# Weight passes tied into program order, and a different start of the first pair, in a one-core attention and two-layer kernel

## The chip, the cores and the metric

The kernel runs on one core of a Trainium2 chip. The metric is the device time of one execution in microseconds (us); lower is better. Five engines work side by side, each through its own list of instructions in a fixed order: TensorE (PE in the profile, its weight loads PEld), VectorE (DVE), ScalarE (ACT), GpSimd (POOL) and SyncE (SP), which here issues every transfer. An instruction whose input is not there yet holds up all that stand behind it in its engine's list.

## The reference

```python
def _attn_ref(q, k, v):                       # 4 batches, 8 heads, 1152 rows, 64 wide
    q_pool = q.reshape(B, H, S // 2, 2, D).mean(axis=3)
    scores = 1.0 / np.sqrt(D) * np.matmul(q_pool, k.transpose(0, 1, 3, 2))
    attn = np.exp(scores - np.max(scores, axis=-1, keepdims=True))
    attn = attn / (np.sum(attn, axis=-1, keepdims=True) + 1e-09)
    return np.matmul(attn, v)                 # 576 rows a head
...
x = attention, laid out as 2304 tokens x 512
h = x @ w_in;   g = h * np.cos(h);                  x = g @ w_out     # 512 x 2048 x 512
h = x @ w_in2;  g = h * (1.0 / (1.0 + np.exp(-h))); return g @ w_out2
```

The weights arrive as 64-bit numbers, q, k and v as 32-bit ones.

## The kernel before

Attention is worked off in 16 pairs of heads, four to a batch. A pair has nine tiles of query rows, so a batch has 36 tiles. Ahead of its tiles, `pair_prep` takes the largest magnitudes of q, k and v (`absmax`, L121 in the profile), makes power-of-two scales from them through a small product with a constant matrix on TensorE (`scale_steps`, tile `bm`, L105 to L116), splits q, k and v into a high and a low half in 16 bits on ScalarE and VectorE (`qn`, `kn`, `vt`; L481 to L485, L436, L441), and has q and k transposed by transfers (`qT`, `kT`). For each tile TensorE makes the scores (`sp`, L521), VectorE copies them out with their minimum (`sc`, L540, two instructions a tile, the first 512 wide; then `nb`, L545), ScalarE takes the exponential (L548) and the high half (`hl`, L554), GpSimd the low half (L559), a transfer transposes both (`hlT`, L561), and TensorE multiplies with v (`pv`, L572 and L576). There are four `sc` buffers, and one comes free when GpSimd has made the low half. After every three tiles VectorE closes a group (`den`, L584).

While the first batch runs, the first layer's weights are prepared in 16 pieces of 1 MB (`layer1_weight_steps`): eight of `w_in`, then eight of `w_out`. A piece is loaded into one of three buffers (`wst`, L180). It has two ScalarE instructions (L196, L197), three VectorE passes over 1024 columns (L198, L202, L206), called weight passes below, a small product for its scale (`mw`, `bm`), two more ScalarE instructions (L219, L220) and one on GpSimd (L221). The next load waits until the third pass has freed its buffer. No first-layer product (`h`, L657) can start before half of the first batch's last pair is through; from then on attention and first layer share the engines. The second layer follows.

The order of each engine's list is set when the program is built: a scheduler issues what it takes to be ready, by a priority that is the place in the code. `W1_TABLE = (6, (0, 2, 4, 8, 11))` says at which steps of the code a piece's parts are written down: piece i at 6i, its parts at the offsets; a tile has four such steps. The scheduler may issue a part earlier than that, when its inputs are there.

```python
s, u = w.si, w.ui                              # one scale a piece
sc = scale_steps(m, pspool(), (s, u), 14, True, True, True)
```

The product tile `bm` comes from a pool of two TensorE accumulation buffers (`ps_h`), which the pairs' scales and the weight pieces' scales share.

Of the kernel before, what the change touches and what calls it, by code (L numbers as in the profile page):

```python
# [26 lines left out]
PSH = 15.0  # L27
# [3 lines left out]
W1_TABLE = (6, (0, 2, 4, 8, 11))  # L31
# [17 lines left out]
def attention_moe_moe_kernel(ctx, tc, q, k, v, w_in1, w_out1, w_in2, w_out2, out):  # L49
# [34 lines left out]
    def scale_steps(m, pool, res, top, wide=False, apart=False, clean=False):  # L84
# [5 lines left out]
        if wide:  # L90
            w = small.tile([128, 1], F32, name="mw", tag="mw")
            wi, mi = w.bitcast(I32), m.bitcast(I32)
            nc.vector.tensor_scalar(
                out=wi, in0=mi, scalar1=3, scalar2=EXP_MASK if clean else 0x3F800000, op0=ALU.logical_shift_left,
                op1=ALU.bitwise_and
            )
# [8 lines left out]
        nc.tensor.matmul(bc[:, 0:n], mean, m, start=True, stop=True)  # L105
# [12 lines left out]
        )  # L118

# [45 lines left out]
    def layer1_weight_steps(w, srcs, stage, pspool, eng, bufs, wt_bufs, period, offs):  # L165
# [20 lines left out]
        def piece_steps(kind, p):  # L186
# [9 lines left out]
            nc.scalar.activation(out=t, in_=hf, func=AF.Abs, scale=2.0**16)  # L196
            nc.scalar.activation(out=low, in_=high16, func=AF.Identity, scale=2.0**-13, bias=floor3)  # L197
            nc.vector.tensor_scalar(  # L198
                out=t, in0=t, scalar1=W_MIN * 2.0**16, scalar2=None, op0=ALU.max, op1=ALU.max, accum_out=m
            )  # L200
            yield
            nc.vector.scalar_tensor_tensor(  # L202
                out=ti, in0=ti, scalar=3, in1=low, op0=ALU.logical_shift_left, op1=ALU.bitwise_or
            )
            yield
            nc.vector.scalar_tensor_tensor(  # L206
                out=ti, in0=st[:, :, :, 1], scalar=-(1 << 31), in1=ti, op0=ALU.bitwise_and, op1=ALU.bitwise_or
            )
# [3 lines left out]
            sc = scale_steps(m, pspool(), (s, u), 14, True, True, True)  # L212
# [17 lines left out]
        for _ in range(bufs):  # L230
            more()
        yield
        events = []
        for i, x in enumerate(pieces):
            g = []
            events += [(i * period + o, len(events) + k, x, g) for k, o in enumerate(offs)]
        events.sort(key=lambda x: x[:2])
        now = 0
        for when, _, x, g in events:
# [3 lines left out]
            if not g:  # L243
                g.append(piece_steps(*x))
# [198 lines left out]
    def pair_prep(at, P):  # L443
# [9 lines left out]
        for i in range(2):  # L453
            absmax(m[:, 3 + i:4 + i], P.v[i], AX.XY)
            yield
        m3 = small.tile([128, 3], F32, name="pm3", tag="pm3")
        nc.vector.tensor_copy(m3[:, 0:1], m[:, 0:1])
        nc.vector.tensor_reduce(
            out=m3[:, 1:3], in_=m[:, 1:5].rearrange("p (a b) -> p a b", b=2), axis=AX.X, op=ALU.max
        )  # L460
# [41 lines left out]
        for i in range(2):  # L502
            do_v(i)
            yield
# [737 lines left out]
```

## Time and profile before

| | before |
|---|---|
| median of 3 runs | 1375.48 us (1375.44 to 1376.28) |
| profiled execution: its own time | 1377.37 us |
| profiled execution: span of the core | 1375.3 us |
| busy share of the span: PE, DVE, ACT, POOL | 84%, 76%, 63%, 45% |
| transfers: share of 16 engines' span | 65% |
| mean granted TensorE clock | 0.917 |

The span runs from the first to the last recorded instruction; the rest of an execution's own time lies around it. Busy shares are means over stages with different limits. The granted clock is a share of full speed (2.4 GHz); the profile shows it per stretch.

### The profile page before, as it was taken

Reading aid. Unit: us, or ns where it says so; the run is one execution under the profiler, and the core shown is the slowest. Engines: PE = TensorE matmul, PEld = TensorE weight load, DVE = VectorE, ACT = ScalarE, POOL = GpSimd, SP = SyncE. Lnnn points to the kernel's source line nnn. Section 1 sums busy time; section 2 is a strip of 40 time slices with the busy share of each in tenths; the row PEclk is TensorE's granted clock in tenths of the full one; section 3 lists DMA queues with packets and bytes.
Section 4 is the critical chain, followed back from the end, with each engine's and each line's share of the span. In section 5 each row is a group of like instructions: output and inputs, shape, how many; then the busy total and the mean of one; then the engine's idle time right before and its main releaser. Section 6 shows DMA issues by size and latency. Waiting matters only on the chain. (4 is left out here: it accounts for less than half of the span.)

```text
span 1375.3 us, 26440 instructions
## 1 busy us (share of the span) xinstructions
PE 1152.2 (84%) x10668; PEld 917.7 (67%) x10668; DVE 1046.8 (76%) x1927; ACT 871.6 (63%) x1061; POOL 624.3 (45%) x352
## 2 busy tenths in 40 slices
PE   1554656888998778888898889998999999999998
PEld 0232334566776556665676668787788888888887
DVE  7799988798887979986898996786757755444483
ACT  4868878578777778886688765634546634433352
POOL 2475867456566465655377553352667500000000
PEclk9756758888999889998999999999999999999999
DMA  9989999987799999998899966422345000000001
GB/s 289 204 160 241 243 210 179 176 166 134 143 212 176 199 195 209 173 164 176 152 198 202 208 116 126 102 91 55 85 93 131 31 24 24 17 16 16 17 31 31
DMA packets 509593, 186.26 MB, mean 135 GB/s; under 512 B 465952, under 2 KB 484384, under 8 KB 509472
## 3 DMA queue, kind: packets, MB, share of 16 engines
q1 hardware_dynamic: 509472, 184.59, 65.0%
q8 instruction: 83, 1.36, 0.4%
q14 instruction: 38, 0.31, 0.1%
HBM read 66.58 MB, written 9.44 MB: 55 GB/s over the span
## 5 line engine op out<-in xcount | busy, mean ns | idle before, releaser
L559 POOL TENSOR_TENSOR hl<-sc,hl 128x1152 f16<-128x1152 f32 x144 | 370.1, 2581 | 170.1 <-ACT hl L554 94.2
L521 PE MATMUL sp<-kT,qT 128*128 128x512 f16 (+1 forms) x768 | 198.3, 377 | 102.8 <-DVE sc L540 91.8
L540 DVE TENSOR_SCALAR_CACHE_REDUCE sc<-sp,psu 128x512 f32<-128x512 f32 (+1 forms) x288 | 228.6, 808 | 48.4 <-PE sp L521 43.4
L657 PEld LDWEIGHTS <-ih 128*128 128x128 f16 x2304 | 226.7, 100 | 44.2 <-issue 12.9
L572 PE MATMUL pv<-vt,hlT 128*128 128x130 f16 (+1 forms) x1440 | 197.9, 239 | 54.0 <-DMA hlT<-hl 45.1
L548 ACT ACTIVATE sc<-sc,nb 128x1152 f32<-128x1152 f32 x144 | 179.7, 1250 | 82.3 <-DVE nb L545 59.2
L572 PEld LDWEIGHTS <-hlT 128*128 128x128 f16 (+1 forms) x1440 | 148.0, 111 | 92.3 <-DMA hlT<-hl 64.4
L657 PE MATMUL h<-ys,ih 128*128 128x256 f16 x1152 | 195.6, 274 | 4.1 <-ACT gs L673 4.1
L521 PEld LDWEIGHTS <-qT 128*128 128x128 f16 x768 | 77.3, 109 | 167.0 <-issue 130.8
L657 PE MATMUL h<-xT,ih 128*128 128x256 f16 x1024 | 187.8, 278 | 0.7 <-DMA xT<-xn 0.6
L576 PE MATMUL pv<-vt,hlT 128*128 128x65 f16 (+1 forms) x1440 | 188.3, 209 | 0.0
L554 ACT ACTIVATE hl<-sc 128x1152 f16<-128x1152 f32 x144 | 164.7, 1154 | 26.7 <-DMA hlT<-hl 13.3
L712 PE MATMUL y<-gh,oh 128*128 128x256 f16 x576 | 162.9, 283 | 7.8 <-ACT y L721 7.1
L712 PE MATMUL y<-gl,oh 128*128 128x256 f16 x576 | 163.0, 283 | 0.4 <-POOL gl L701 0.4
L712 PE MATMUL y<-gh,ol 128*128 128x256 f16 x576 | 162.8, 283 | 0.0
L826 PEld LDWEIGHTS <-op 128*128 128x128 f16 x1512 | 147.9, 98 | 18.0 <-issue 0.6
L657 PE MATMUL h<-ys,il 128*128 128x256 f16 x576 | 157.8, 274 | 0.0
L576 PEld LDWEIGHTS <-hlT 128*128 128x128 f16 (+1 forms) x1440 | 144.7, 109 | 19.3 <-issue 11.4
L657 PE MATMUL h<-xT,il 128*128 128x256 f16 x512 | 141.9, 277 | 0.0
L701 POOL TENSOR_TENSOR gl<-tt,gh 128x1024 f16<-128x1024 f32 x36 | 93.7, 2603 | 92.5 <-DVE gh L700 82.1
L712 PEld LDWEIGHTS <-oh 128*128 128x128 f16 x1152 | 114.9, 102 | 28.5 <-issue 9.6
L657 PEld LDWEIGHTS <-il 128*128 128x128 f16 x1152 | 114.3, 99 | 15.6
(310 smaller groups left out, 2043.3 us busy)
## 6 DMA issues: line engine op xcount, KB each, us to landing
wst<-in_moe_w_in_dram SPq DMA_DIRECT2D x16, 1024.0 KB, 6.2
stk<-in_k_dram SPq DMA_DIRECT2D x32, 288.0 KB, 4.0
stv<-in_v_dram SPq DMA_DIRECT2D x32, 288.0 KB, 4.1
stq<-in_q_dram SPq DMA_DIRECT2D x32, 256.0 KB, 3.2
wst<-in_moe_w_out_dram SPq DMA_DIRECT2D x8, 1024.0 KB, 6.2
wst<-in_moe_w_out_dram SPq DMA_DIRECT2D x16, 512.0 KB, 6.1
ydr<-y SPq DMA_DIRECT2D x9, 512.0 KB, 3.3
y32b<-ydr SPq DMA_DIRECT2D x9, 512.0 KB, 3.3
```

The source lines that it names most:

```text
L521: nc.tensor.matmul(sp[:, o - a:o - a + n], P.qT[e][:, t, :], kT[:, o:o + n], start=(e == 0), stop=(e == 1))
L540: nc.vector.tensor_scalar(out=T.sc[:, a:z], in0=sp, scalar1=T.P.su, scalar2=None, op0=ALU.mult, op1=ALU.min, accum_out=mx[:, x:x + 1],)
L548: nc.scalar.activation(out=T.sc, in_=T.sc, func=AF.Exp, scale=-1.0, bias=nb)
L554: nc.scalar.activation(out=hi, in_=T.sc, func=AF.Copy)
L559: nc.gpsimd.tensor_tensor(out=T.hl[:, 1, :], in0=T.sc, in1=T.hl[:, 0, :], op=ALU.subtract)
L572: nc.tensor.matmul(G.pv[r, T.gi], T.hlT[:, 0, c, r], P.vt[i][:, c], start=(c == 0), stop=(c == KC - 1), skip_group_check=True,)
L576: nc.tensor.matmul(G.pv[r, T.gi, 0], T.hlT[:, 1, c, r], P.vt[i][:, c, 0], start=False, stop=(c == KC - 1), skip_group_check=True,)
L657: nc.tensor.matmul(hp, wt[:, c, f * 128:(f + 1) * 128], xt(c), start=(i == 0), stop=(i == 3 * NC - 1), skip_group_check=True,)
L701: nc.gpsimd.tensor_tensor(out=G.gl, in0=t, in1=gh, op=ALU.subtract)
L712: nc.tensor.matmul(blk.y[:, oc, :], wt[:, f, oc * 128:(oc + 1) * 128], gt[:, f % 4, :], start=(f == 0 and e == 0 and oc % 2 == 0), stop=(f ...
L826: nc.tensor.matmul(bank, t[:, e, c, :], wt[:, c, :], start=start, stop=True, skip_group_check=True)
```

## The change

It has four parts. In the diff, `pin` (the scheduler's `keep_in_program_order`) lets the scheduler issue an instruction only behind the one that was written down just ahead of it for the same engine.

1. A one-element exponential of a constant (`warm`) is issued on ScalarE at the start; the instruction that loads ScalarE's function table then stands in front of it and no longer in front of `qn`.
2. For the first pair alone, v's maxima and scale are taken out of the common scale and get a product of their own (`pmv`, `pmm`, `psv`); q and k's product has two columns instead of three.
3. In front of the first pair, two weight pieces instead of three are started (the new last number of `W1_TABLE`); the third load is written down behind the first pair's preparation.
4. All other parts of the weight pieces, from the scale on for the first two, are pinned.

```diff
-W1_TABLE = (6, (0, 2, 4, 8, 11))
+W1_TABLE = (6, (0, 2, 4, 8, 11), 2)
...
         nc.vector.memset(halfpi, math.pi / 2)
+        nc.scalar.activation(out=small.tile([128, 1], F32, name="warm", bufs=1), in_=halfpi, func=AF.Exp)
...
-        nc.tensor.matmul(bc[:, 0:n], mean, m, start=True, stop=True)
+        put(nc.tensor.matmul(bc[:, 0:n], mean, m, start=True, stop=True))
...
+    pin = tc.keep_in_program_order
...
-            nc.scalar.activation(out=t, in_=hf, func=AF.Abs, scale=2.0**16)
+            put(nc.scalar.activation(out=t, in_=hf, func=AF.Abs, scale=2.0**16))
...
-            sc = scale_steps(m, pspool(), (s, u), 14, True, True, True)
+            sc = scale_steps(m, pspool(), (s, u), 14, True, True, True, pin)
...
-            nc.scalar.activation(out=hi, in_=t, func=AF.Copy, scale=s)
-            nc.scalar.activation(out=t, in_=t, func=AF.Copy, scale=s)
-            nc.gpsimd.tensor_tensor(out=lo, in0=t, in1=hi, op=ALU.subtract)
+            pin(nc.scalar.activation(out=hi, in_=t, func=AF.Copy, scale=s))
+            pin(nc.scalar.activation(out=t, in_=t, func=AF.Copy, scale=s))
+            pin(nc.gpsimd.tensor_tensor(out=lo, in0=t, in1=hi, op=ALU.subtract))
...
-        for _ in range(bufs):
+        for _ in range(first):
             more()
         yield
+        for _ in range(bufs - first):
+            more()
         events = []
         for i, x in enumerate(pieces):
             g = []
-            events += [(i * period + o, len(events) + k, x, g) for k, o in enumerate(offs)]
+            if i < first:
+                g.append(piece_steps(*x, lambda ins: ins))
+                for _ in range(2):
+                    next(g[0])
+            events += [(i * period + o, len(events) + k, x, g) for k, o in enumerate(offs) if i >= first or k >= 2]
+        yield
...
-                g.append(piece_steps(*x))
+                g.append(piece_steps(*x, pin))
...
+        if apart:
+            nc.vector.tensor_reduce(out=m3[:, 1:2], in_=m[:, 1:3], axis=AX.X, op=ALU.max)
+            run_all(scale_steps(m3[:, 0:2], ps_h, (s[:, 0:2], u[:, 0:2]), 12))
...
+        def v_scale():
+            mv = small.tile([128, 2], F32, name="pmv", bufs=1)
+            for i in range(2):
+                absmax(mv[:, i:i + 1], P.v[i], AX.XY)
+            mm = small.tile([128, 1], F32, name="pmm", bufs=1)
+            nc.vector.tensor_reduce(out=mm, in_=mv, axis=AX.X, op=ALU.max)
+            sv_, uv_ = (small.tile([128, 1], F32, name=nm, bufs=1) for nm in ("psv", "puv"))
+            run_all(scale_steps(mm, ps_h, (sv_, uv_), 12))
+            return sv_
...
+        P.sv = v_scale() if apart else sv
...
-                run_all(pair_prep(at, P[0]))
+                run_all(pair_prep(at, P[0], True))
+                next(wg)
```

The changed kernel's lines have higher numbers: L198, L202, L206 become L201, L205, L209, L540 becomes L565, L554 becomes L579, L219 and L220 become L222 and L223. In the built lists the 48 weight passes stand on VectorE, counted between the first score copies (512 wide) of the tiles named, as follows: ahead of tile 0 there were 8 and are now 6; from there to tile 9 (pair one's first) 10 and now 5; to tile 18 (pair two's first) 15 and now 13; to tile 27 (pair three's first) 12 and now 19; behind it 3 and now 5. On SyncE three weight loads still stand in front, in the same place. Of the 16 loads, 7 stood ahead of the transpose of tile 2, 3 more ahead of that of tile 9, 4 more ahead of tile 18's and the last 2 ahead of tile 27's; now it is 5, 2, 5 and 4.

VectorE's list from the first pair to the first score copy, the last twelve rows of before (three weight passes, two L198 and one L202, stand ahead of them, behind the first pair's `vt`):

```order
L121 TENSOR_REDUCE pm<-stk 128x1
L206 SCALAR_TENSOR_TENSOR wt<-wst,wt 128x1024
L108 TENSOR_SCALAR ui_76<-bm 128x1
L202 SCALAR_TENSOR_TENSOR wt<-wt,wst 128x1024
L93 TENSOR_SCALAR mw<-wm 128x1
L198 TENSOR_SCALAR wt,wm<-wt 128x1024
L112 TENSOR_SCALAR si_75<-ui_76 128x1
L206 SCALAR_TENSOR_TENSOR wt<-wst,wt 128x1024
L202 SCALAR_TENSOR_TENSOR wt<-wt,wst 128x1024
L116 TENSOR_SCALAR ui_76<-ui_76 128x1
L93 TENSOR_SCALAR mw<-wm 128x1
L540 TENSOR_SCALAR sc,mx<-sp,psu 128x512
```

The same stretch of VectorE's list in the changed kernel, whole, right behind the first pair's `vt`:

```order
L201 TENSOR_SCALAR wt,wm<-wt 128x1024
L205 SCALAR_TENSOR_TENSOR wt<-wt,wst 128x1024
L201 TENSOR_SCALAR wt,wm<-wt 128x1024
L209 SCALAR_TENSOR_TENSOR wt<-wst,wt 128x1024
L94 TENSOR_SCALAR mw<-wm 128x1
L124 TENSOR_REDUCE pm<-stk 128x1
L205 SCALAR_TENSOR_TENSOR wt<-wt,wst 128x1024
L209 SCALAR_TENSOR_TENSOR wt<-wst,wt 128x1024
L94 TENSOR_SCALAR mw<-wm 128x1
L565 TENSOR_SCALAR sc,mx<-sp,psu 128x512
```

Two passes and the first piece's scale moved behind the first score copy.

ScalarE's list in pair zero, from pair one's splits to the fourth tile's `hl`, before:

```order
L548 ACTIVATE sc<-sc,nb 128x1152
L481 ACTIVATE qn<-stq,ps__293 128x9x64 x2
L436 ACTIVATE kn<-stk,ps__293 128x9x64 x2
L219 ACTIVATE ih_82<-wt,si_75 128x4x256
L436 ACTIVATE vt<-stv,ps__293 128x9x64 x2
L554 ACTIVATE hl<-sc 128x1152
L548 ACTIVATE sc<-sc,nb 128x1152
L219 ACTIVATE ih_82<-wt,si_75 128x4x256 x2
L197 ACTIVATE wst<-wst,floor_74 128x1024
L548 ACTIVATE sc<-sc,nb 128x1152
L220 ACTIVATE wt<-wt,si_75 128x1024
L554 ACTIVATE hl<-sc 128x1152
```

The same stretch of ScalarE's list in the changed kernel:

```order
L505 ACTIVATE qn<-stq,ps__270 128x9x64 x2
L446 ACTIVATE kn<-stk,ps__270 128x9x64 x2
L446 ACTIVATE vt<-stv,ps__270 128x9x64 x2
L579 ACTIVATE hl<-sc 128x1152
L222 ACTIVATE ih_82<-wt,si_75 128x4x256
L573 ACTIVATE sc<-sc,nb 128x1152
L222 ACTIVATE ih_82<-wt,si_75 128x4x256
L573 ACTIVATE sc<-sc,nb 128x1152
L223 ACTIVATE wt<-wt,si_75 128x1024
L579 ACTIVATE hl<-sc 128x1152
```

Five weight instructions stood there and three do now; up to the fourth `hl`, counted from the list's start, 17 did and 7 do now.

VectorE's list near the change from pair two to pair three, before (tile 26's copies and the start of pair four's maxima):

```order
L540 TENSOR_SCALAR sc,mx<-sp,psu 128x512
L198 TENSOR_SCALAR wt,wm<-wt 128x1024
L540 TENSOR_SCALAR sc,mx<-sp,psu 128x640
L202 SCALAR_TENSOR_TENSOR wt<-wt,wst 128x1024
L93 TENSOR_SCALAR mw<-wm 128x1
L545 TENSOR_SCALAR nb<-mx 128x1
L206 SCALAR_TENSOR_TENSOR wt<-wst,wt 128x1024
L121 TENSOR_REDUCE pm<-stk 128x1
L121 TENSOR_REDUCE pm<-stv 128x1
L108 TENSOR_SCALAR uo_78<-bm 128x1
L121 TENSOR_REDUCE pm<-stv 128x1
L112 TENSOR_SCALAR so_77<-uo_78 128x1
```

VectorE's list in the changed kernel, twelve rows out of the 37 between tile 26's last score copy and tile 27's first (`pu__1358` and `ps__1357` are pair three's scales):

```order
L201 TENSOR_SCALAR wt,wm<-wt 128x1024
L205 SCALAR_TENSOR_TENSOR wt<-wt,wst 128x1024
L209 SCALAR_TENSOR_TENSOR wt<-wst,wt 128x1024
L94 TENSOR_SCALAR mw<-wm 128x1
L109 TENSOR_SCALAR uo_78<-bm 128x1
L113 TENSOR_SCALAR so_77<-uo_78 128x1
L109 TENSOR_SCALAR pu__1358<-bm 128x3
L117 TENSOR_SCALAR uo_78<-uo_78 128x1
L113 TENSOR_SCALAR ps__1357<-pu__1358 128x3
L117 TENSOR_SCALAR pu__1358<-pu__1358 128x3
L480 TENSOR_SCALAR psu<-pu__1358 128x1
L506 SCALAR_TENSOR_TENSOR qn<-stq,ps__1357,qn 128x9x64
```

Pair three's scale now stands behind a weight piece's scale, and its splits stand behind all of pair two's score copies; before, its splits (`qn`, `kn`) stood among the copies of tiles 25 and 26. Pair two's splits moved in the same way, from the copies of tiles 12 to 14 to behind tile 17's. In this stretch of 37 rows stand ten weight passes.

## Rows read from the trace of the kernel before

**Rows 1.** Busy time by stretch: length, PE, PEld, DVE, ACT, POOL, clock, DMA share, GB/s.

```profile
0.00:29.77 29.77, 3.25 (x10) 1.90 (x11) 20.14 (x38) 14.07 (x15) 4.99 (x15) 1.00 0.94 274
29.77:85.77 56.00, 27.09 (x144) 14.69 (x144) 46.56 (x102) 38.66 (x40) 31.30 (x13) 0.72 0.80 190
85.77:145.66 59.89, 31.33 (x265) 20.39 (x264) 55.35 (x114) 51.19 (x56) 38.81 (x19) 0.67 1.12 237
145.66:196.29 50.63, 33.55 (x277) 21.46 (x275) 46.06 (x107) 42.60 (x48) 33.40 (x20) 0.67 1.11 228
196.29:234.43 38.14, 23.32 (x190) 14.10 (x190) 33.60 (x79) 28.66 (x36) 30.09 (x14) 0.77 0.92 175
234.43:262.20 27.77, 20.77 (x216) 13.34 (x214) 23.77 (x61) 19.98 (x22) 19.69 (x13) 0.81 1.05 205
262.20:1057.00 794.80, 701.15 (x6724) 553.47 (x6724) 641.21 (x1170) 541.88 (x659) 447.51 (x245) 0.94 0.78 154
1057.00:1375.30 318.30, 311.69 (x2853) 278.33 (x2850) 180.06 (x267) 134.52 (x187) 18.48 (x17) 1.00 0.07 23
```

**Rows 2.** Timeline of the first pair: start, duration, engine, instruction, [idle before, releaser].

```profile
9.03 1.45 DVE L121 TENSOR_REDUCE pm<-stv 128x1 f32<-128x576 f32 x2
...
10.73 0.59 PE L105 MATMUL bm<-pm,mean 128*128 128x3 f32 x2 [10.73 <-DVE pm L458]
11.36 0.16 DVE L108 TENSOR_SCALAR pu__151<-bm 128x3 f32<-128x3 f32 x1 [0.68 <-PE bm L105]
11.55 0.17 DVE L112 TENSOR_SCALAR ps__150<-pu__151 128x3 int32<-128x3 int32 x1
...
11.79 1.28 ACT L481 ACT_TABLE_LOAD   x1 [11.79 <-DMA wst<-in_moe_w_in_dram]
...
13.08 1.44 ACT L481 ACTIVATE qn<-stq,ps__150 128x576 f16<-128x576 f32 x2
13.89 0.82 DVE L482 SCALAR_TENSOR_TENSOR qn<-stq,ps__150,qn 128x576 f16<-128x576 f32 x1 [1.72 <-ACT qn L481]
...
19.74 2.73 SPq L497 DMA_TRANSPOSE kT<-kn  x1
...
24.39 2.08 PE L521 MATMUL sp<-kT,qT 128*128 128x512 f16 x6 [2.89 <-DMA kT<-kn]
...
27.30 2.43 DVE L202 SCALAR_TENSOR_TENSOR wt<-wt,wst 128x1024 int32<-128x1024 int32 x1
...
29.77 0.73 DVE L540 TENSOR_SCALAR_CACHE_REDUCE sc<-sp,psu 128x512 f32<-128x512 f32 x1
```

**Rows 3.** Groups of instructions on VectorE, 0 to 262 us: weight passes.

```profile
L202 DVE SCALAR_TENSOR_TENSOR wt<-wt,wst 128x1024 int32<-128x1024 int32 x16 | 29.9, 1866 | 0.3 <-DVE uo L108 0.2
L206 DVE SCALAR_TENSOR_TENSOR wt<-wst,wt 128x1024 int32<-128x1024 int32 x16 | 28.9, 1804 | 0.0
L198 DVE TENSOR_SCALAR_CACHE_REDUCE wt<-wt 128x1024 f32<-128x1024 f32 x16 | 19.3, 1208 | 0.0
```

**Rows 4.** Timeline of pair zero, 54 to 70 us, all engines.

```profile
54.10 2.17 ACT L219 ACTIVATE ih<-wt,si 128x1024 f16<-128x1024 f32 x2
...
61.66 2.18 ACT L220 ACTIVATE wt<-wt,si 128x1024 f32<-128x1024 f32 x2
...
64.44 0.22 DVE L584 TENSOR_SCALAR den<-pv,ps__150 128x3 f32<-128x3 f32 x1 [6.49 <-PE pv L576]
...
67.39 4.21 POOL L221 TENSOR_TENSOR il<-wt,ih 128x1024 f16<-128x1024 f32 x2
...
69.55 0.74 DVE L540 TENSOR_SCALAR_CACHE_REDUCE sc<-sp,psu 128x512 f32<-128x512 f32 x1
```

**Rows 5.** Timeline of SyncE, one transpose, about 113 us.

```profile
113.09 6.61 SPq L487 DMA_TRANSPOSE qT<-qn  x1
```

**Rows 6.** Timelines of GpSimd and VectorE, 71 to 83 us.

```profile
71.56 11.32 POOL L559 TENSOR_TENSOR hl<-sc,hl 128x1152 f16<-128x1152 f32 x4
...
77.38 3.27 DVE L206 SCALAR_TENSOR_TENSOR wt<-wst,wt 128x1024 int32<-128x1024 int32 x1
```

More of the change, by code (lines that the diff above doesn't have):

```diff
@@ L163, in new_w, with layer1_weight_steps @@
         return w
-    def layer1_weight_steps(w, srcs, stage, pspool, eng, bufs, wt_bufs, period, offs):
+    def layer1_weight_steps(w, srcs, stage, pspool, eng, bufs, wt_bufs, period, offs, first):
         npc = w.npc
@@ L184, in more, with piece_steps @@
             staged.append(st)
-        def piece_steps(kind, p):
+        def piece_steps(kind, p, put):
             st = staged.pop(0)
@@ L195, in piece_steps @@
             high16 = st.rearrange("p c f z -> p c (f z)").bitcast(U16).rearrange("p c (f z) -> p c f z", z=4)[:, :, :, 1]
[L196 to L198 removed]
+            put(nc.scalar.activation(out=t, in_=hf, func=AF.Abs, scale=2.0**16))
+            put(nc.scalar.activation(out=low, in_=high16, func=AF.Identity, scale=2.0**-13, bias=floor3))
+            put(nc.vector.tensor_scalar(
                 out=t, in0=t, scalar1=W_MIN * 2.0**16, scalar2=None, op0=ALU.max, op1=ALU.max, accum_out=m
[L200 removed]
+            ))
             yield
[L202 removed]
+            put(nc.vector.scalar_tensor_tensor(
                 out=ti, in0=ti, scalar=3, in1=low, op0=ALU.logical_shift_left, op1=ALU.bitwise_or
[L204 removed]
+            ))
             yield
[L206 removed]
+            put(nc.vector.scalar_tensor_tensor(
                 out=ti, in0=st[:, :, :, 1], scalar=-(1 << 31), in1=ti, op0=ALU.bitwise_and, op1=ALU.bitwise_or
[L208 removed]
+            ))
             more()
@@ L452, in pair_prep @@
         yield
-        for i in range(2):
-            absmax(m[:, 3 + i:4 + i], P.v[i], AX.XY)
-            yield
+        s = small.tile([128, 3], F32, name="ps_", tag="ps_", bufs=3)
+        u = small.tile([128, 3], F32, name="pu_", tag="pu_", bufs=3)
         m3 = small.tile([128, 3], F32, name="pm3", tag="pm3")
         nc.vector.tensor_copy(m3[:, 0:1], m[:, 0:1])
-        nc.vector.tensor_reduce(
-            out=m3[:, 1:3], in_=m[:, 1:5].rearrange("p (a b) -> p a b", b=2), axis=AX.X, op=ALU.max
-        )
-        s = small.tile([128, 3], F32, name="ps_", tag="ps_", bufs=3)
-        u = small.tile([128, 3], F32, name="pu_", tag="pu_", bufs=3)
-        yield from early(scale_steps(m3, ps_h, (s, u), 12), P_CH)
-        P.s = s
+        sv = s[:, 2:3]
+        if apart:
+            nc.vector.tensor_reduce(out=m3[:, 1:2], in_=m[:, 1:3], axis=AX.X, op=ALU.max)
+            run_all(scale_steps(m3[:, 0:2], ps_h, (s[:, 0:2], u[:, 0:2]), 12))
+        else:
+            for i in range(2):
+                absmax(m[:, 3 + i:4 + i], P.v[i], AX.XY)
+                yield
+            nc.vector.tensor_reduce(
+                out=m3[:, 1:3], in_=m[:, 1:5].rearrange("p (a b) -> p a b", b=2), axis=AX.X, op=ALU.max
+            )
+            yield from early(scale_steps(m3, ps_h, (s, u), 12), P_CH)
         P.su = small.tile([128, 1], F32, name="psu", tag="psu", bufs=3)
@@ L469, in pair_prep @@
         P.vt = [None] * 2
+        def v_scale():
+            mv = small.tile([128, 2], F32, name="pmv", bufs=1)
+            for i in range(2):
+                absmax(mv[:, i:i + 1], P.v[i], AX.XY)
[4 more added lines that the diff above has]
+            return sv_
         def do_v(i):
@@ L584, in group_end @@
         nc.vector.tensor_scalar(
-            out=den[:, 0:n], in0=G.pv[:, 0:n, 0, D:D + 1], scalar1=1e-9 * 2.0**PSH, scalar2=G.P.s[:, 2:3],
+            out=den[:, 0:n], in0=G.pv[:, 0:n, 0, D:D + 1], scalar1=1e-9 * 2.0**PSH, scalar2=G.P.sv,
             op0=ALU.add, op1=ALU.mult,
```

10 lines of the change are left out of this document (5 added, 5 removed).

## The prediction

> **What bounds the kernel now.** I read the busy time by stretch first, cut where the first score copy of each pair of the first batch falls [rows 1]. The reader sees three regimes. In the last 318 us TensorE is busy for 311.7 at full clock: nothing edited here works there. From 262 to 1057 us TensorE (701 of 795) and VectorE (641) share the load, and the edit only shifts that stretch, unless the new order costs it something. The first 262 us, where the edit works, belong to no single engine: VectorE is busy 20.1 of 29.8 us in front, 46.6 of 56.0 in pair zero, 55.4 of 59.9 in pair one, 46.1 of 50.6 in pair two. Transfers run at a share of 1.12 and 1.11 in pairs one and two, which I read as full, but at 0.80 in pair zero. So pair zero is where time is lost to waiting: 9.4 us of VectorE.
>
> Second the timeline, for who ends those waits. In front [rows 2], v's two maxima (1.45) stand ahead of the common product at 10.73; scales are written at 11.55; then ScalarE loads its table for 1.28 us before `qn` starts at 13.08. The scores are being made from 24.39, yet VectorE takes the first at 29.77: it is busy with weight passes, so it is VectorE's list and not the transposes that sets that moment. In pair zero [rows 4] VectorE stands for 6.49 us at `den`, which waits for `pv`, that for a transpose, that for GpSimd's low half, and that for ScalarE's `hl`; around it ScalarE is doing weight instructions (two in 2.17 us, two in 2.18), and GpSimd two weight pieces (4.21) while score buffers wait for it. The next tile's score copy comes only at 69.55.
>
> **The change part by part.** All 48 weight passes are still done; at the unhindered 1.21 us of [rows 3] I count where they go: two leave the front, five pair zero, two pair one; seven come to pair two and two to pair three. That is -2.4, -6.1, -2.4, +8.5, +2.4, sum zero. What is left is idle time won or lost, stretch by stretch.
>
> *Front.* One of v's maxima no longer stands ahead of the product, the other runs beside it (0.73 saved against the product's 0.63, less 0.16 for a small reduction that comes between): -0.55. The table is loaded while ScalarE has nothing else (it is idle until 11.79): -1.28. The added VectorE steps of v's own scale are four of 0.16, and lie in the 1.72 us in which VectorE waits for `qn` anyway; if that cover shrinks they cost up to 0.6. The added product (0.59) has an idle TensorE. Beside the two moved passes, the first score copy is also rid of a pass that took 2.43 (1.2 more than unhindered) and of three small steps (0.4). Net of moved work: -3.4; the first score copy at 29.77 - 5.8 = 24.0. The scores are there, at 24.39 - 1.8 = 22.6 and half a microsecond of product. Bounds: 0, if the weight pieces land no earlier than they do now, and -3.4. I take -3.4, because VectorE has no gap from 13.89 on. The third piece's load is not moved: on SyncE's list it stands where it stood, so that edit costs and gains nothing by itself.
>
> For the table, the Trainium skill ("ScalarE: Activation LUTs", section "What ACT_TABLE_LOAD costs") counts a load and a drain, 2.66 us in all; here the row shows 1.28 and `qn` right behind it, on an engine that had nothing to drain. By the page's figure the front would win 1.4 more; the measured row decides.
>
> *Pair zero.* Up to the fourth `hl`, ScalarE has ten weight instructions fewer ahead, at some 1.1 us each [rows 4]; four of them stood between the first exponential and that `hl`. So `hl`, low half, transpose and `pv` come earlier relative to VectorE's list. Bounds for the 9.4 idle microseconds: none won (another input of the same chain, the transposes, ends it), all won. I take 5, about three quarters of the 6.49 wait.
>
> *Pair one into pair two.* Pair two's splits now stand behind all of pair one's score copies. Behind its `kn` VectorE has v's split (two of 0.8), a group end (0.9 by estimate) and three passes (3.6): 6.1 us of cover. Against it stand the transposes: from the issue of `kT` to the first product 4.65 us, plus a microsecond in which `qT` is still being issued and half a microsecond of product [rows 2], 6.2. That would be even; but with transfers full an issue of a transpose can take 6.61 [rows 5]. Bounds 0 and +6; I take +2.
>
> *Pair two into pair three.* Here the order empties the pipeline: some 37 rows with ten passes and no score copy. On ScalarE about twelve instructions of 1.1 stand ahead of pair three's `qn` (13), then `qn` and `kn` (2.8), VectorE's last low half (0.8), the rest of the transposes (5.7) and half a microsecond: 23. VectorE meanwhile has ten passes (12.1), the splits (4.2) and some 3.5 of small steps and group ends: 20. So +3, and up to +7 with a slow transpose. Queued behind the waiting VectorE are tile 27's copies, and behind those ScalarE and GpSimd, whose backlog has run out. Of the 4.6 idle microseconds that pair two has now, the additional passes fill some: -2 (0 to -4).
>
> *Stretch.* The 32 passes with two inputs in on-chip memory cost 29.9 + 28.9 = 58.8 us [rows 3] where 32 at 1.21 would be 38.7; one took 3.27 beside GpSimd's low halves [rows 6]. How many coincide after the change no row tells; six of the ten passes in the block above are of this kind and run when GpSimd has few low halves left, at 0.6 less each, while others meet more of them. I take -1, with -6 and +6 as bounds.
>
> Sum: -3.4 - 5 + 2 + 3 - 2 - 1 = -6.4 us. All of it should reach the end, because behind 262 us the same work is done in nearly the same order. Against the profiled execution: span 1375.3 - 6.4 = 1368.9, with 2.1 around it 1371.0; its own time was 1.9 above the median, so **1369.1**. Less than 0.2% (2.75 us) cannot be told from no change here.
>
> **The rivals.** *More is won.* Pair zero is freed to the rate of its transfers: 0.80 of 56.0 is 44.8, at a share of 1.12 it takes 40 us, 16 less, of which 6.1 is moved work; and the starts of pairs two and three find transposes fast and cost nothing. -3.4 - 10 - 1 = -14.4: 1361. For it speaks that ScalarE is only 38.7 of 56 busy there; against it, that transfers never were full in the stretches with few loads.
>
> *Nothing is won.* What pairs zero and one gain is lost again at the two starts: +2 becomes +5 and +3 becomes +5, no filling: -3.4 - 5 + 5 + 5 - 1 = +0.6, some 1375 to 1376. For it: pairs one and two are already full of transfers, and two loads more go into pair two's part than before.
>
> *Slower.* One mechanism: pair three's scale waits behind the weight pieces' scales. Its product shares two buffers with theirs, and pinned pieces come late; each step of VectorE's list there (a pass, then a product, then a scale) waits for ScalarE first. If both starts meet transposes as in [rows 5], they cost +6 and +7 and nothing is filled: -3.4 - 5 + 13 = +4.6, 1380. It decides from the point at which the two starts together cost more than 9.4. Against it: ten passes do stand in that gap.
>
> *Passes collide.* Nine passes go where tiles are denser; if their six with two inputs all took the 3.27 of [rows 6] and not the mean 1.84 of [rows 3], that is +8.6 on -6.4: about 1378. The Trainium skill ("SBUF — State Buffer", section "Who interferes with whom") says that a VectorE instruction with two inputs in that memory and a GpSimd instruction that reads it exclude each other for their whole length. The trace agrees: [rows 6] shows such a pass at 3.27, and the one-input pass of [rows 3] stays at its 1.21.
>
> **How the numbers follow.** Forecast 0.42 (own range 1364 to 1372.7), more won 0.20, nothing won 0.18, pair starts 0.15, collisions 0.05. Faster is 0.62, same 0.18, slower 0.20. The range reaches from just short of the rival with more (1360) to just short of the slower one (1379).
>
> **What would show it.** In the profile after: `qn` at about 11.2 and the table load near 1 us; the first score copy near 24; no wait of 6 us at `den`; pair one's first copy some 17 us earlier than 85.77 (5.8 in front, 6.1 moved, 5 won); the first copies of pairs two and three 17 and 8 us earlier than now, because the passes come back there, and a VectorE wait for products ahead of each; then a constant lead to the end. I am wrong if the lead at pair one is under 10 us, if waits ahead of pairs two and three exceed 9 us together, or if the lead of the first 262 us is not kept behind it.

## The result, and the profile after

The changed kernel took 1383.38 us (median of 7 runs, 1381.94 to 1388.46) against 1376.28 us of the kernel before in the same runs: a ratio of 1.006 (95% interval 1.0044 to 1.0076). It is slower by 0.6%, where 1369.1 us and a gain were forecast. The profiled execution took 1383.38 us, its span is 1381.4 us, the mean granted clock 0.921.

The busy time by stretch of the changed kernel, cut at the same events as [rows 1] (the first score copies of tiles 0, 9, 18, 27 and 36, the first h product), columns as there:

```profile
0.00:25.57 25.57, 2.23 (x7) 1.51 (x8) 16.91 (x36) 9.84 (x12) 2.01 (x13) 1.00 0.95 271
25.57:72.49 46.92, 27.74 (x156) 15.12 (x155) 40.18 (x89) 36.97 (x39) 26.82 (x12) 0.76 0.98 229
72.49:125.41 52.92, 32.30 (x310) 22.84 (x309) 47.03 (x102) 44.74 (x53) 36.09 (x20) 0.73 1.10 225
125.41:196.21 70.80, 35.99 (x292) 24.66 (x291) 60.24 (x129) 53.12 (x60) 43.72 (x23) 0.60 1.05 223
196.21:242.78 46.57, 25.79 (x180) 14.90 (x179) 42.03 (x89) 33.63 (x35) 30.55 (x13) 0.62 0.67 150
242.78:267.05 24.27, 13.86 (x152) 8.80 (x152) 20.75 (x53) 14.84 (x18) 13.80 (x11) 0.93 1.01 189
```

Against [rows 1] the stretches are 4.2, 9.1 and 7.0 us shorter up to pair two, 20.2 longer in pair two and 8.4 longer in pair three, and 3.5 shorter up to the first h product. So a lead of 20.3 us at tile 18 is down to 0.1 us at tile 27, and at tile 36 the changed kernel is 8.4 us late. Behind the first h product it loses another 1.2. The sum, 6.1 us, is the difference of the spans (1381.4 and 1375.3).

Half of pair two's stretch is one gap: tile 26's first score copy is at 160.11, tile 27's at 196.21, 36.1 us later (before: 187.22 and 196.29, 9.1 us). The same view of that gap alone shows no engine full (VectorE 28.3 of 36.1, TensorE 12.6) and a clock of 0.54:

```profile
160.11:196.21 36.10, 12.63 (x135) 10.67 (x132) 28.32 (x51) 27.04 (x33) 20.10 (x12) 0.54 0.99 207
```

The timeline of the gap, rows of VectorE, ScalarE, TensorE, SyncE and GpSimd in order of time:

```profile
144.02 0.15 DVE L475 TENSOR_REDUCE pm<-pm 128x2 f32<-128x4 f32 x1
...
160.11 0.74 DVE L565 TENSOR_SCALAR_CACHE_REDUCE sc<-sp,psu 128x512 f32<-128x512 f32 x1
160.56 0.36 PE L106 MATMUL bm<-mw,mean 128*128 128x1 f32 x2
160.90 0.87 DVE L565 TENSOR_SCALAR_CACHE_REDUCE sc<-sp,psu 128x640 f32<-128x640 f32 x1
...
166.93 0.59 PE L106 MATMUL bm<-mw,mean 128*128 128x1 f32 x2 [1.82 <-DVE mw L94]
...
171.22 0.22 DVE L609 TENSOR_SCALAR den<-pv,ps__790 128x3 f32<-128x3 f32 x1 [3.14 <-PE pv L601]
...
174.64 3.27 DVE L209 SCALAR_TENSOR_TENSOR wt<-wst,wt 128x1024 int32<-128x1024 int32 x1
176.80 5.19 POOL L224 TENSOR_TENSOR ol<-wt,oh 128x1024 f16<-128x1024 f32 x2
177.84 0.14 DVE L94 TENSOR_SCALAR mw<-wm 128x1 int32<-128x1 int32 x1
178.03 0.59 PE L106 MATMUL bm<-mw,mean 128*128 128x1 f32 x2 [6.84 <-DVE mw L94]
178.45 8.09 SPq L586 DMA_TRANSPOSE hlT<-hl  x2
178.48 0.57 PE L106 MATMUL bm<-pm,mean 128*128 128x3 f32 x2
...
179.28 0.64 DVE L113 TENSOR_SCALAR ps__1357<-pu__1358 128x3 int32<-128x3 int32 x1
179.96 2.05 DVE L117 TENSOR_SCALAR pu__1358<-pu__1358 128x3 int32<-128x3 int32 x1
180.09 1.43 ACT L505 ACTIVATE qn<-stq,ps__1357 128x576 f16<-128x576 f32 x2
...
186.63 3.54 SPq L511 DMA_TRANSPOSE qT<-qn  x1
190.27 2.75 SPq L521 DMA_TRANSPOSE kT<-kn  x1
...
192.07 0.22 DVE L609 TENSOR_SCALAR den<-pv,ps__790 128x3 f32<-128x3 f32 x1 [2.80 <-PE pv L601]
...
194.93 2.08 PE L546 MATMUL sp<-kT,qT 128*128 128x512 f16 x6 [2.89 <-DMA kT<-kn]
...
203.82 2.84 POOL L584 TENSOR_TENSOR hl<-sc,hl 128x1152 f16<-128x1152 f32 x1 [4.42 <-issue]
206.69 16.56 SPq L586 DMA_TRANSPOSE hlT<-hl  x4
```

The reader is to see three things. Pair three's maxima are reduced at 144.02, its scale is written at 179.28: 35.3 us for a step that needs one product of 0.57 us. The product stands in TensorE's list behind those of three weight pieces in these rows (160.56, 166.93 and 178.03). The last of them waits for `mw`, and so for that piece's three passes, and these stand on VectorE's list behind `den`, which waits 3.14 us for a `pv` of pair two. Then, from the scale on, ScalarE's `qn`, VectorE's splits and SyncE, which is still issuing two `hlT` transposes until 186.54, take another 17 us to the first copy. By then no tile is under way: GpSimd's next low half comes at 203.82, the next `hlT` transpose at 206.69, and the share of transfers falls to 0.67 in pair three's stretch (0.92 in [rows 1]).

In the kernel before, the same step took 20.8 us, but ended 18 us ahead of tile 26's first copy (187.22), in time for tile 27:

```profile
147.98 0.14 DVE L458 TENSOR_REDUCE pm<-pm 128x2 f32<-128x4 f32 x1
...
168.78 1.62 DVE L112 TENSOR_SCALAR ps__1397<-pu__1398 128x3 int32<-128x3 int32 x1
```

The edits in front did what they were meant to. Timeline of the changed kernel up to the first score copy (beside [rows 2]), and its wait at `den` in pair zero (beside [rows 4]):

```profile
0.73 1.28 ACT L79 ACT_TABLE_LOAD   x1 [0.73 <-PEq L1252]
...
11.34 1.44 ACT L505 ACTIVATE qn<-stq,ps__145 128x576 f16<-128x576 f32 x2 [9.11 <-DVE ps__145 L113]
...
25.57 0.75 DVE L565 TENSOR_SCALAR_CACHE_REDUCE sc<-sp,psu 128x512 f32<-128x512 f32 x1 [1.08 <-PE sp L546]
...
56.88 0.22 DVE L609 TENSOR_SCALAR den<-pv,psv 128x3 f32<-128x3 f32 x1 [3.52 <-PE pv L601]
```

`qn` starts 1.74 us earlier. The first copy now waits for scores, which it did not before: it is the transposes, and no longer VectorE's list, that set that moment (`kT` was issued at 19.81, hardly other than the 19.74 of [rows 2]; the issue of `qT` ahead of it took 6.13).

### The profile page after: what moved, and what is told of

It is laid out like the page before. It is cut to its first block, busy times and chain, and to the rows that moved or that the text cites. A ratio compares the mean times of both kernels' runs of the same rounds, so it can differ in the third digit from the quotient of the medians.

```text
span 1381.4 us, 26435 instructions
## 1 busy us (share of the span) xinstructions
PE 1148.4 (83%) x10670; PEld 918.3 (66%) x10670; DVE 1051.0 (76%) x1931; ACT 871.3 (63%) x1062; POOL 622.6 (45%) x352
## 5 line engine op out<-in xcount | busy, mean ns | idle before, releaser
L546 PE MATMUL sp<-kT,qT 128*128 128x512 f16 (+1 forms) x768 | 193.8, 369 | 101.3 <-DVE sc L565 69.7
L565 DVE TENSOR_SCALAR_CACHE_REDUCE sc<-sp,psu 128x512 f32<-128x512 f32 (+1 forms) x288 | 229.5, 807 | 40.4 <-PE sp L546 38.3
L682 PE MATMUL h<-xT,ih 128*128 128x256 f16 x1024 | 191.5, 279 | 3.1 <-DMA xT<-xn 3.0
L579 ACT ACTIVATE hl<-sc 128x1152 f16<-128x1152 f32 x144 | 164.7, 1154 | 11.5 <-DMA xT<-xn 4.0
```

Of the source, the lines that this page charges most:

```text
L546: nc.tensor.matmul(sp[:, o - a:o - a + n], P.qT[e][:, t, :], kT[:, o:o + n], start=(e == 0), stop=(e == 1))
L565: nc.vector.tensor_scalar(out=T.sc[:, a:z], in0=sp, scalar1=T.P.su, scalar2=None, op0=ALU.mult, op1=ALU.min, accum_out=mx[:, x:x + 1],)
L579: nc.scalar.activation(out=hi, in_=T.sc, func=AF.Copy)
L682: nc.tensor.matmul(hp, wt[:, c, f * 128:(f + 1) * 128], xt(c), start=(i == 0), stop=(i == 3 * NC - 1), skip_group_check=True,)
```

## The experiments

**Theory 1:** a pair's scale product and the weight pieces' scale products share the two `bm` buffers of `ps_h`; where pieces stand late, the pair's product queues behind theirs, its splits come too near to its first tile, and the pipeline drains. **Theory 2:** the weight passes put off from the front have to be done ahead of the first h product in any case, so a lead is given back wherever they land. The ratios below are each against the kernel before, run beside it on the same chip. Runs of one kernel spread by 6 to 20 us there, so a ratio is known to 0.2 or 0.3%. A mark is the first score copy of a tile or the first h product, read from one trace; a gap is the time between the first copies of two neighbouring tiles; a lead is how much earlier a mark comes than in the first trace of the kernel before.

### A buffer of its own for one of the two products

Run `e_ownbuf` is the changed kernel with the pieces' product in the second stage's buffer, which is idle until the first h product:

```diff
-        bc = pool.tile([128, 2, GW], F32, tag="h", name="bm")[:, 0, 0:4]
+        bc = (ps_y.tile([128, NC, GW], F32, tag="y", name="bm") if pool is None else pool.tile([128, 2, GW], F32, tag="h", name="bm"))[:, 0, 0:4]
...
-                wg = layer1_weight_steps(W1, (w_in1, w_out1), wst, lambda: ps_h, nc.sync, W1_BUFS, WT_BUFS, *W1_TABLE)
+                wg = layer1_weight_steps(W1, (w_in1, w_out1), wst, lambda: None, nc.sync, W1_BUFS, WT_BUFS, *W1_TABLE)
```

> The changed kernel with one edit: the scale product of a weight piece goes into the buffer of the h sums' second stage, which is idle until 262 us, and no longer into the two buffers that it shares with the scale product of a pair. Theory 1 (the scale product of pairs two and three stands behind the scale products of the tied weight pieces in those two buffers, and so the pair's splits, transposes and scores start late): the gap of 36 us between the first score copies of tiles 26 and 27 goes back to below 15 us, the lead over the kernel before at tile 27, now 0.1 us, becomes 10 us or more, and the time is 1362 to 1372 us. Theory 2 (the weight passes that were put off have to be done in pair two's stretch in any case, whichever buffer the pair's product uses): the lead at tile 27 stays below 5 us, and the time is 1378 us or more. In between, both have a share.

Measured: 1377.99 us, ratio 0.9999 (0.9979 to 1.002). Tile 27's first copy is at 179.23, a lead of 17.1 us, and the gap ahead of it 7.9 us. The timeline of VectorE in this kernel, pair three's last reduction of maxima and its scale:

```profile
140.49 0.14 DVE L476 TENSOR_REDUCE pm<-pm 128x2 f32<-128x4 f32 x1
...
146.60 0.62 DVE L114 TENSOR_SCALAR ps__1357<-pu__1358 128x3 int32<-128x3 int32 x1
```

6.1 us in place of 35.3, counted from the same reduction: theory 1 named the place. It did not have the time, which is 6 us above its range and at the edge of theory 2's, and the lead does not last. Its busy time by stretch, pairs two and three:

```profile
119.57:179.23 59.66, 34.49 (x305) 23.06 (x304) 47.60 (x114) 49.40 (x57) 41.13 (x23) 0.66 1.04 222
179.23:231.69 52.46, 29.30 (x251) 20.24 (x250) 46.39 (x99) 43.04 (x49) 33.29 (x16) 0.73 0.99 204
```

Pair three's stretch is 14.3 us longer than in [rows 1]; it holds 11 weight passes, 3 before. Eight passes at the means of [rows 3] (1.63 over the three kinds) are 13.0 us. So theory 2 holds for what comes behind the gap: at tile 36 2.7 us of the 17.1 are left.

Nor was the lead at tile 27 time won: with the buffer the order changes too, and 34 passes stand ahead of tile 27 here, 45 in the kernel before and 43 in the changed one; eleven passes at 1.63 us are 17.9. What the own buffer is worth is read where all 48 passes are done in each of these kernels. The first h product comes at 260.47, against 267.05 in the changed kernel: 6.6 us, about what the change had lost.

Run `p_pair_own` takes the two products apart from the other side: the pieces' product stays, and that of pairs one to four moves (the first line of the diff above is kept).

```diff
-            yield from early(scale_steps(m3, ps_h, (s, u), 12), P_CH)
+            yield from early(scale_steps(m3, None if P.own else ps_h, (s, u), 12), P_CH)
...
+            P[n].own = n <= 4
             yield from early(slowly(pair_prep(at, P[n]), PREP_PACE[late]), P_PR)
```

> The changed kernel with the shared buffers taken apart from the other side: the weight pieces' scale product stays where it was, and that of pairs one to four goes into the idle buffer. The program order on every engine becomes that of the kernel in which the pieces' product was moved. Theory 1 (the two kinds of product stand in each other's way in two buffers; which of them moves doesn't matter): the gaps ahead of tiles 18 and 27 are below 10 us as there (3.4 and 7.9), the first copy of tile 27 at 177 to 182 us, and a ratio of 0.998 to 1.002. Theory 3 (it is the pieces that gain by another buffer, since their own chain of passes runs earlier): the gap ahead of tile 27 stays above 20 us and the ratio above 1.003.

Measured: 1379.54 us, ratio 1.0013 (0.9994 to 1.0031); gaps of 3.4 and 8.6 us, tile 27 at 179.08, 5.9 us from the reduction to the scale. The first h product comes at 259.69. It makes no difference which of the two moves: it is the sharing. Since the order is the same in both runs, they do not tell the shorter wait apart from the passes that moved with it, and a third buffer in the shared pool was not tried.

### Parts of the change

Run `a_noscalepin` lets loose the two tied steps of a piece's scale:

```diff
-            sc = scale_steps(m, pspool(), (s, u), 14, True, True, True, pin)
+            sc = scale_steps(m, pspool(), (s, u), 14, True, True, True)
```

> The changed kernel with the two tied steps of a weight piece's scale (the exponent pass on VectorE and the product on TensorE) let loose; the five passes ahead and the splits behind stay tied. If these two ties are what holds the pair's product back, the gap ahead of tile 27 falls below 20 us and the time to 1372 us or less. By theory 1 it is the buffers, not these ties: the order moves by one or two passes (18 passes instead of 19 in pair two's stretch), the gap stays at 25 us or more, and the time is 1379 to 1384 us. Theory 2 says the same, so this run speaks on the ties alone.

Measured: 1386.88 us, ratio 1.0053 (1.0032 to 1.0073), gap 28.6 us; the time is above the range that either theory gave. Of the gap of 36.1 us most stays: these two ties alone are not what holds the pair's product.

Run `d_pins_only` has the ties and two pieces in front, without the edits of part 1 and part 2:

```diff
-        nc.scalar.activation(out=small.tile([128, 1], F32, name="warm", bufs=1), in_=halfpi, func=AF.Exp)
...
-                run_all(pair_prep(at, P[0], True))
+                run_all(pair_prep(at, P[0]))
```

> The changed kernel without the table and v's scale: ties and two weight pieces in front alone. Theory 1 and theory 2: the gap ahead of tile 27 stays at 30 us or more, and the time is 1384 to 1389 us, that of the changed kernel plus the 3 to 5 us that the edits in front are worth. If the edits in front are at fault instead, it is 1376 us or less. If the lead from the front is swallowed by the gap ahead of tile 27 anyway, it is within 1 us of the changed kernel, 1383 us.

Measured: 1385.31 us, ratio 1.0043 (1.0019 to 1.0067), gap 38.3 us, tile 36 at 245.11. Ties and two pieces alone make a loss of that size; the interval overlaps that of the changed kernel, so what the front edits are worth beside it isn't read from this run.

Run `c_front_only` has parts 1 and 2 alone, three pieces in front and no ties (the other `pin`s are out too):

```diff
-W1_TABLE = (6, (0, 2, 4, 8, 11), 2)
+W1_TABLE = (6, (0, 2, 4, 8, 11), 3)
...
-                g.append(piece_steps(*x, pin))
+                g.append(piece_steps(*x, lambda ins: ins))
```

> The changed kernel with nothing tied, and with three weight pieces loaded in front as before: the edits of ScalarE's table and of v's scale alone. The theories agree that the loss comes with the ties: the first score copy at 24.5 to 27 us (29.77 before), the first copies of the later pairs 2 to 6 us ahead of the kernel before, no gap above 20 us ahead of any pair, and 1371 to 1375 us. A rival says that a lead won in front is lost behind, whatever the order of the weight passes: then the first copy of tile 27 is within 1 us of before, and the time is 1375.5 to 1377 us.

Measured: 1388.73 us, ratio 1.0058 (1.0038 to 1.0077). Both expectations were wrong. The first copy (26.35) and the gaps (none above 9.5 us) are as forecast, and the lead of 3.4 us at tile 0 is 8.1 at tile 18; but tile 36 comes 11.7 us later than before, with no tie at all. So the front edits alone lose as much as the ties and two pieces alone (1.0043), and the two losses don't add. Two runs take the two edits apart. `j_table_only` is the kernel before with this line alone:

```diff
+        nc.scalar.activation(out=small.tile([128, 1], F32, name="warm", bufs=1), in_=halfpi, func=AF.Exp)
```

> The kernel before with the early activation that loads ScalarE's table alone; the program order on every engine is that of before apart from it. A table load of 1.28 us leaves the front: the first score copy at 28.0 to 29.2 us (29.77 before). If a lead won in front is carried through, 0.5 to 1.5 us are gained, a ratio of 0.999 to 1.000. If the front edits cost time behind by themselves, the ratio is above 1.002.

Measured: 1376.18 us, ratio 0.9982 (0.9959 to 1.0004). The first copy is at 27.30, and the lead of 2.5 us is 1.8 at tile 36: `qn` starts 1.25 us earlier, and the pass of 2.43 us at the end of [rows 2] took 1.21. The interval holds 1, so a gain in time isn't shown. `k_vscale_only` is `c_front_only` without that line:

> The kernel before with v's scale of pair zero from its own product alone, nothing tied, three pieces in front. Its program order is that of the kernel with both edits in front and nothing tied, which was measured at a ratio of 1.0058: 15 weight passes in pair two's part and 12 in pair one's, 12 and 15 in the kernel before, and pair four's splits 3 tiles ahead of its first score copy in place of 5. If that order is what costs, the ratio is 1.004 to 1.008, and tile 36 comes 8 us or more later than before. If v's scale only shortens the front, the ratio is 0.998 to 1.000.

Measured: 1385.87 us, ratio 1.0048 (1.0026 to 1.0071); tile 36 at 243.80, 9.4 us late. v's scale does shorten the front (28.14), but with it the scheduler puts three weight passes out of pair one's part into pair two's, and pair three's scale, reduced at 128.71 and written at 171.18, waits 42.5 us behind weight pieces (20.8 in the kernel before), without a tie. This wait does not empty the pipeline ahead of pair three: the gap ahead of tile 27 is 9.4 us, as before (9.1), and 7.1 of the 9.4 us are lost behind it, in pair three's stretch (45.3 us against 38.1, three weight passes in both). How the loss comes about there the run doesn't show; `h_own_untied`, below, takes the wait and the loss away.

### The own buffer with other orders

`h_own_untied` is `c_front_only` with the buffer of its own, as in the diff of `e_ownbuf`:

> The edits in front, three pieces loaded there, nothing tied, the weight pieces' scale product in its own buffer. In program order the splits of pairs one to four stand 4, 4, 5 and 7 tiles ahead of their pair's first score copy; 12, 14, 14 and no weight passes fall into pairs zero to three. Theory 1: no gap above 10 us ahead of any pair, tile 36 at 228 us or earlier, the first h product at 258 us or earlier, and 1367 to 1374 us, some 15 us below the same kernel without the own buffer. Theory 2: the first h product at 259 to 262 us, so that only the lead of the front is left of it, and 1373 to 1377 us.

Measured: 1374.24 us, ratio 0.9975 (0.9956 to 0.9994). That is 0.8% below the same edits with shared buffers. The scales of pairs three and four wait 5.6 and 5.7 us (the gap ahead of tile 9 is 12.2 us, above theory 1's bound), and tile 36 comes at 238.10, 8.0 us earlier than in `c_front_only`. But that is 3.7 us later than in the kernel before, and the first h product, at 263.59, is later than either theory had it; what it wins over the kernel before comes from behind (below).

`i_before_own` is the kernel before with the buffer of its own, nothing else:

> The kernel before with one edit: the weight pieces' scale product in its own buffer. The splits then stand 4, 4, 4 and 6 tiles ahead of the first score copy of pairs one to four (4, 5, 1 and 5 before). Theory 1: the gap of 9.1 us ahead of tile 27 falls below 6 us, and the time by 3 to 6 us, to a ratio of 0.996 to 0.998. Theory 2: within 0.2% of before.

Measured: 1372.72 us, ratio 0.9961 (0.9944 to 0.9978), gap 4.1 us ahead of tile 27. The size is that of theory 1, the way isn't: tile 36 comes at 240.83, 6.4 us later than before.

`g_own_period5` is `e_ownbuf` with a weight piece every 5 tiles, `g_own_first3` is `e_ownbuf` with three pieces in front:

```diff
-W1_TABLE = (6, (0, 2, 4, 8, 11), 2)
+W1_TABLE = (5, (0, 2, 4, 8, 11), 2)
```

```diff
-W1_TABLE = (6, (0, 2, 4, 8, 11), 2)
+W1_TABLE = (6, (0, 2, 4, 8, 11), 3)
```

> The changed kernel with the weight pieces' scale product in its own buffer, and with a weight piece every 5 tiles in place of 6. In program order the splits of pairs one to four then stand 4, 6, 5 and 7 tiles ahead of their pair's first score copy (4, 0, 0 and 2 in the changed kernel, 4, 5, 1 and 5 before). Theory 1 (what counts is that distance: a pair whose splits come with fewer than 3 tiles to go starts late): no gap above 10 us ahead of any pair, tile 36 copied for the first time at 225 us or earlier (234.43 before), the first h product at 256 us or earlier (262.2 before), and 1366 to 1373 us. Theory 2 (the work that VectorE has to do ahead of the first h product sets its start, 225 of 262 us before, and a lead won early is given back where the passes are put): the lead over the kernel before at tile 36 is under 4 us, the first h product comes at 258 us or later, and the time is 1374 us or more.

Measured: 1376.08 us, ratio 0.999 (0.9972 to 1.0009). The gap ahead of tile 9 was 10.8 us, the others up to 7.6; the lead at tile 36 is 3.2 us. Theory 2 had the time and the lead, theory 1 the first h product (255.54). Early splits alone do not make a faster kernel.

> The changed kernel with the own buffer and with three weight pieces loaded in front, as before the change; the ties stay. The splits stand 4, 6, 7 and 3 tiles ahead of the first score copy of pairs one to four; 8, 4, 12, 12 and 10 weight passes fall ahead of tile 0 and into pairs zero to three. Theory 1: no gap above 10 us ahead of pairs one to three, the first copy of tile 27 some 15 us ahead of before, pair four's (distance 3) within 12 us, and 1368 to 1375 us. Theory 2: pair three's stretch is 10 us longer than before for its 7 passes more, the lead at tile 36 is below 5 us, and the time is 1374 to 1379 us.

Measured: 1388.85 us, ratio 1.0072 (1.0045 to 1.01), beyond both theories, though no gap is above 10 us. Pair three's stretch is 57.5 us. The timelines of GpSimd and SyncE in it show another wait of the same make:

```profile
216.51 2.87 POOL L585 TENSOR_TENSOR hl<-sc,hl 128x1152 f16<-128x1152 f32 x1
232.22 1.41 POOL L457 TENSOR_TENSOR stq<-stq 128x576 f32<-128x576 f32 x1 [12.85 <-DMA stq<-in_q_dram]
...
228.49 0.58 SPq L437 DMA_DIRECT2D stq<-in_q_dram  x1
```

A load of the next pair's q was issued at 228.49 only, behind three transposes on SyncE's list; GpSimd's addition, already in its list, waited 12.85 us for it, and the low halves stood behind that. There a product waited for its place in a list, here a load.

### A second trace, and a version that beats both

The unedited kernels once more:

> The changed kernel once more, unedited, for a second trace and for a ratio on the chip of the experiments. If the marks are set by the program order, the gap ahead of tile 27 is 36 us within 3, the first score copy of tile 36 at 240 to 245 us, and the ratio 1.004 to 1.008. If the marks are a matter of chance in one execution, tile 36 is off by more than 5 us from 242.78.

> The kernel before once more, unedited, for a second trace. If its marks are set by the program order, the first score copies of tiles 9, 18, 27 and 36 come within 2 us of 85.77, 145.66, 196.29 and 234.43; the spread that is found says how small a lead can be read.

The changed kernel: 1382.09 us, ratio 1.0033 (1.0004 to 1.0061), gap 38.4 us, tile 36 at 245.25; the ratio is just below what was expected and the mark just above. The kernel before (one run, 1380.13 us): tiles 9, 27 and 36 within 0.4 us of their places in the first trace, tile 18 within 2.5. In two traces of each kernel the marks up to tile 36 agree to within 2.5 us, so a lead smaller than that is uncertain. What follows differs more: from tile 36's first copy to the last tile's, the changed kernel took 590.4 us in its first trace and 581.2 in its second, the kernel before 594.5 and 596.7. So of the 8 to 10 us that it is late at tile 36 it wins back some, a different amount each time.

`n_own_table` is `i_before_own` with the `warm` line:

> The kernel before with the two edits that measured best by themselves: the early table load (ratio 0.998) and the weight pieces' scale product in its own buffer (0.996). If they add up: the first score copy at 27.3 to 28.5 us, the marks up to tile 36 some 2 us ahead of the kernel with the own buffer alone, and a ratio of 0.993 to 0.996. If the lead of the front is lost behind, 0.996 to 0.998.

Measured: 1371.02 us, ratio 0.9959 (0.9937 to 0.9982): faster than the kernel before and the changed one. Up to tile 36 it is 1.6 to 4.1 us ahead of `i_before_own`, but at 0.9959 to 0.9961 the two can't be told apart. Where the 0.4% of both come from is open. It isn't the gap: they are behind the kernel before at tile 36 (236.74 and 240.83 against 234.43), and then take 587.9 and 585.1 us to the last tile's first copy; `h_own_untied` takes 586.0, the kernel before 594.5 and 596.7, `j_table_only` 596.8. In that stage the same products keep TensorE busy for 494 to 496 us in the first three and 507 to 510 us in the other three traces, and in the stretch from tile 36 to tile 54 the granted clock is 0.91 to 0.93 against 0.85 to 0.90. It is no accident of one trace: the medians of the mean granted clock over all runs are 0.936, 0.932 and 0.929 for these three, 0.922 and 0.923 for the kernel before beside them. But it isn't the own buffer alone: `e_ownbuf` has it, and a median of 0.920 and 595.5 us in that stage, while the changed kernel, with shared buffers, took 581.2 in its second trace and `d_pins_only` 586.2. Whether the clock is the cause or follows from a denser stream no run tells.

## Why the prediction was wrong

*The step that failed* is "Pair two into pair three": +3, "up to +7 with a slow transpose", with -2 for filling. Beyond the 8.5 us of moved passes pair two's stretch grew by 11.7: VectorE's idle time went up from 4.6 to 10.6 us instead of down, and the other 5.7 are work beyond the count. The prediction set two chains side by side, 23 us through ScalarE and the transposes against 20 us of VectorE's cover. From the end of tile 26's last copy (161.77) to tile 27's first the block took 34.4 us. `qn` started after 18.3 us (13 in the prediction), because pair three's scale stood behind the product of a tied piece, and that piece's passes behind pair two's last groups on VectorE. From `qn` to the copy it took 16.1 us (9.8 in the prediction): the splits were done at 183.34 for q, but two `hlT` held SyncE until 186.54, a queue that the sum had left out. The cover was too small as well: VectorE was busy for 26.7 us of the block, its ten passes took 15.4 (12.1 counted) and the splits 6.3 (4.2), and it still stood idle for 7.8, most of it at `den` (3.14 and 2.80).

*The mechanism had been named*, as the rival "Slower": "pair three's scale waits behind the weight pieces' scales. Its product shares two buffers with theirs". It was given 0.15, against it the argument that ten passes stand in the gap anyway. Its price, +7 for that start, was a slow transpose and not this wait; by the sum's own terms the rival also lacks the -1 of the stretch. Runs `e_ownbuf` and `p_pair_own` show the sharing to be the cause of the gap. The length of the wait by itself is not the price, as the 20.8 us of the kernel before and the 42.5 of `k_vscale_only` show, neither with a long gap; by these traces what counts is how far it reaches past the last tiles of the pair in front.

*A term was missing.* An emptied pipeline has to fill again: with two passes more, pair three's stretch grew by 8.4 us, 6.0 beyond the passes, while the share of transfers was 0.67. The sum had "a constant lead" from there. That all of the 6.0 is the filling isn't shown.

*The other terms.* The front gave 4.2 us of lead, not 5.8 (1.8 beside the moved passes, not 3.4): `qn` and the table were right (11.34 and 0.73), but the transposes took over as the limit. Pair zero won 3.0 beside its moved passes, not 5; the wait at `den` went from 6.49 to 3.52. "Pair one into pair two" was +2 and came out at -4.6: pair two's late splits cost a gap of 16.8 us ahead of tile 18 (9.5 before), but the stretch as a whole had less to do (VectorE busy for 47.0 us, 55.4 before). The term for the stretching of passes was right (-0.8 for the 32 passes, 58.0 against 58.8; -1 forecast). Nor did the load of the third piece cost anything that a row shows. "All of it should reach the end" holds for neither sign: 8.4 us late at tile 36 were 6.1 at the end. Beside the moved passes the measured sum is -1.8 - 3.0 - 4.6 + 11.7 + 6.0 up to tile 36, -3.5 to the first h product and +1.2 behind it: +6.0, where -6.4 had been added up.

*The conditions that were set* tell where it broke: the lead at pair one held (13.3 us, 10 were asked for); the gaps ahead of pairs two and three grew by 7.3 and 27.0 us, and VectorE stood idle in them for 3.3 and 7.8 us (1.3 and 0.2 before), where waits of 9 together were to be too much.

## What to carry to other kernels

Where two kinds of work take turns in one small pool of buffers, a change in the order of the one sets when the other may start: look in each engine's list for what stands ahead of the first step of the next pair (here a product of half a microsecond that waited 35 us), and ask whether it comes before the last tiles of the pair in front are done. Count work that is put off as work at the place where it lands; a lead that was won by putting it off is not one. And an edit that only shortens a step in front can move a scheduler's whole list: read the list behind it before pricing it at its own size, as with v's scale, which saved 1.6 us in front and cost 0.48% in all.

## What had not been expected of the hardware

Two small VectorE instructions in the pair's chain were stretched; in [rows 2] the same scale step took 0.17 us. In the timeline of the gap pair three's scale took 0.64 (until 179.92) and the step behind it 2.05 (179.96 to 182.01), with GpSimd at two weight low halves from 176.80 for 5.19 us. The first low half ended at 179.90 and the second at 181.98, so each VectorE step ended 0.03 us behind one of them. Both read a single input of three columns, so the rule for two inputs that the prediction cited does not cover them. The same section of the Trainium skill ("SBUF — State Buffer", section "Who interferes with whom") says that a `tensor_scalar` can enter a mode in which it contends with GpSimd, and that whoever issues first then holds the shared ports for the whole instruction; the ends agree, but which mode these two ran in no run shows.

The table load cost 1.28 us and nothing behind it also where it was moved to the start: the exponential that needed it began at 2.03, right at its end, and `qn` at 11.34 needed no load again. The drain that the Trainium skill ("ScalarE: Activation LUTs", section "What ACT_TABLE_LOAD costs") adds to a load is seen in neither place.
